# Twelve pair copies issued by SyncE in two earlier stages, and one staging tile given up for a resident pair

## The chip, the cores and the metric

The kernel runs on one core of one Trainium2 chip. The core has a matrix engine (TensorE, PE in the profile; PEld is its weight load), a vector engine (VectorE, DVE), a scalar engine (ScalarE, ACT), a general engine (GpSimd, POOL), a synchronising engine that mostly issues transfers (SyncE, SP), and 16 DMA engines that carry all transfers. The metric is the device time of one execution in microseconds (us); lower is better. It is given as the median of several runs. One more execution is taken with a profiler, and all views shown here come from such executions.

## The reference

Two independent computations are made on the same launch, and their results are put side by side. The first (A) is a state-space convolution: a four-tap shift filter along the sequence of k, times v, then a causal convolution of length 2048 per channel by way of Fourier transforms, then a product with q. The second (B) is an attention layer that carries eight memory rows from one segment of 32 rows to the next, through 64 segments.

```python
# A: S = 2048, D = 1024
for t in range(ks):
    k_shift = k_shift + k_pad[:, t:t + S, :] * shift_k[:, ks - 1 - t][None, None, :]
kv = k_shift * v
y = irfft(rfft(kv padded to 2S) * rfft(ssm_k padded to 2S))[:S] + kv * ssm_D
a = q * y
# B: 32 heads of 128, 8 memory rows, segments of 32 rows
for s in range(n_seg):
    h = jnp.concatenate([mem, xs], axis=1)
    q, k, v = h Wq, h Wk, h Wv
    p = softmax(where(mask, q k^T * scale, -1e9))
    o = (p v) Wo
    mem = o[:, :M, :]
    outs.append(o[:, M:, :])
return jnp.concatenate([a, b], axis=-1)
```

## The kernel before

All of A is computed first, and in its gaps the parts of B that do not depend on the memory rows (the projections of eight of the 32 rows of each segment, called rows in the code). Then the segment loop of B runs, one segment after the other, because each needs the memory rows of the one before.

**Weights of B.** The four weight matrices are cut into pairs of 512 KB: for Wq and Wk, the same 128 x 1024 block of both ("qk"); for Wv, two neighbouring blocks ("v"); for Wo, the rows of two heads ("o"). Not all fit into the on-chip memory (SBUF). Most pairs are resident: they are loaded once, by `res_half` (L119), two halves of 256 KB each, and stay for the whole loop. `open_res(n)` makes room for the next n of them on the left side of SBUF as the tiles of A on the right side are given back, and `load_to` (L149 for the pairs that are not resident, L119 for the resident ones) asks for the halves in the order in which the projections need them; it stops where a pair has no room yet. Two pairs are parked in PSUM. The remaining 17 pairs are streamed: they are loaded anew in every segment into a ring of five tiles, `wring` (L691). The five streamed "v" pairs are read from Wv itself. For the other 12 (seven "qk", five "o") a packed copy is first made in DRAM, `Wst`, and the ring reads that copy. The function `relay(n)` issues the copies of the next n such pairs, two transfers of 256 KB each, from DRAM to DRAM.

**Stages of A.** Times are those of the profiled execution.
1. The filter's stage, up to about 68 us. `k_iter(t)` for t = 0 to 16: the filter kernel ssm_k is transposed (PE, L450), copied to `kt`, and `stage1` of the tile before multiplies it by a table of sines and cosines (L227); ACT and DVE copy the product from PSUM into `s_sb`, and for every second t SP stores 1 MB of it into the DRAM tensor SK (L234). The tables are computed in the same time, mostly on DVE, ACT and POOL.
2. The shift products, about 68 to 165 us. A loop over t = 0, 2, ..., 16. For t below 16, DVE makes eight large operations for two rows of the sequence (L502, L506) and the product with v (L510). SP loads the k rows of a later pair (`load_k`, L251) in the middle of them and v of two rounds ahead (`load_v`, L256) after them. Then PE runs the projections of B in small portions (`rows.half`, L178 for v and L181 for q and k, with their loads on SP by `load_to`), and between them `stage1` of the products of the round before, stored into SU (L234).
3. Stage 2, about 167 to 282 us. For 17 sets, each in two halves (34 units): SP gathers the set from SK and SU (`Kg`, `Ug`, L539), PE transforms it (L567), ACT copies the filter's part (L578, L579), DVE makes the four products (L590), POOL and DVE combine them (Yre L593, Yim L594), PE transforms back (L603), ACT copies the result into a staging tile `zs` (L606), three of which take turns, and SP stores a full set into SZ (L547). Portions of `rows.half` stand between. From the unit i = 12 on, `relay(1)` is called after every second unit; its two transfers go out on POOL's queue (L128). At the end the gather tiles are given back, six more pairs are opened, and their loads follow.
4. Stage 3, about 288 to 358 us. For 16 tiles SP loads `zt` from SZ (L650) and `qt` from q (L652), PE transforms (y_ps, L668), DVE multiplies by q (L671), SP stores the result (L677). Portions of `rows.half` and their loads stand between; ACT stores the projections of a finished q and k block (QKBd, 2 MB, L189).

Then come the last projections, the parked pairs, and from about 388 us the segment loop, up to about 2060 us, and a last product with Wo.

**Order.** The program is scheduled by hand: each engine runs its instructions in the order of the program. A transfer is issued by an engine's queue in that order, too: what it has to wait for (data, a free tile, or the landing of an earlier transfer on the same one of SP's eight semaphores) holds all that stands behind it in that queue.

The lines that the change touches are the issue in `relay`, its one call in stage 2, the call `open_res(3)` ahead of stage 2 and `open_res(6)` ahead of stage 3, and the number of `zs` tiles:

```python
                zs_of[st] = wk.tile([128, 2, 1024], BF, tag="zs", name="zs", bufs=3)
            if i >= 12 and i % 2 == 0:
                relay(1)
```

Of the kernel before, what the change touches and what calls it, by code (L numbers as in the profile page):

```python
# [9 lines left out]
BF = mybir.dt.bfloat16  # L10
# [11 lines left out]
def fused_kernel(ctx: ExitStack, tc, q, k, v, shift_k, ssm_k, ssm_D, outa, x, mem0, Wq, Wk, Wv, Wo, outb, n_seg):  # L22
# [11 lines left out]
    nc = tc.nc  # L34
# [30 lines left out]
    Wst = {key: dram.tile([128, 2, 1024], BF, name=f"Wst{key[0]}{key[1]}_{key[2]}")[:] for key in relaid}  # L65
# [4 lines left out]
    def half_src(key, n):  # L70
        m, g, i = key
        if m == "qk":
            return (Wq, Wk)[n][i * 128:(i + 1) * 128, g * 1024:(g + 1) * 1024]
        if m == "v":
            return Wv[i * 128:(i + 1) * 128, (2 * g + n) * 1024:(2 * g + n + 1) * 1024]
        h = 8 * g + 2 * i + n
        return Wo[h * 128:(h + 1) * 128, :]
# [27 lines left out]
    def open_res(n):  # L105
        if n:
            pool = cw_.enter_context(tc.tile_pool(name=f"b_wres{len(to_open)}", bufs=1))
            if not wide:
                wide["t"] = pool.tile([128, 8, 2, 1024], BF, name="Wearly")
            for _ in range(n):  # L110
                res_pool[to_open.pop(0)] = pool
# [10 lines left out]
    def relay(n):  # L122

        for _ in range(n):
            if relaid:
                key = relaid.pop(0)
                for i in range(2):
                    nc.gpsimd.dma_start(Wst[key][:, i, :], half_src(key, i))  # L128


    class Rows:
# [87 lines left out]
    def stage1(u_tile, t, sbs, scratch, pool, ps_pool, by):  # L219

        if t % 2 == 0:
            sbs[0] = pool.tile([128, 2, 2, 1024], BF, tag="s1_sb", name="s1_sb")
        sb = sbs[0]
        for h in range(2):
            pt = ps_pool.tile([128, 1024], F32, tag="big", name="s1_ps")
            for hf in range(2):
                nc.tensor.matmul(pt[:, hf * 512:(hf + 1) * 512], lhsT=F1h[h][:, :],  # L227
                                 rhs=u_tile[:, hf * 512:(hf + 1) * 512], start=True, stop=True)
            if by[h] == "A":
                nc.scalar.copy(sb[:, h, t % 2, :], pt[:])  # L230
            else:
                nc.vector.tensor_copy(sb[:, h, t % 2, :], pt[:])
        if t % 2 == 1:
            nc.sync.dma_start(scratch.rearrange("m (h r) d -> m h r d", h=2)[:, :, t - 1:t + 1, :], sb[:])  # L234
# [29 lines left out]
    with ExitStack() as ck:  # L264
        ksn = ck.enter_context(tc.tile_pool(name="a_ksn", bufs=1, side="right"))
        KS = ksn.tile([128, 8, 2048], BF, name="KS_nat")
        wk = ck.enter_context(tc.tile_pool(name="a0_wk", bufs=2, side="right"))
# [178 lines left out]
        def k_iter(t):  # L446
            if t < 16:
                k_tp = ps_t.tile([128, 1024], BF, tag="tp", name="k_tp")
                for db in range(8):
                    nc.tensor.transpose(k_tp[:, db * 128:(db + 1) * 128],  # L450
                                        KS[:, db, :].rearrange("p (n r) -> p r n", r=16)[:, t, :], ident[:])
                kts[t] = wk.tile([128, 1024], BF, tag="kt", name="kt")
                if t % 2 == 0:
                    nc.scalar.copy(kts[t][:], k_tp[:])
                else:
                    nc.vector.tensor_copy(kts[t][:], k_tp[:])
                if t == 0:
                    nc.vector.tensor_tensor(out=kts[t][0:1, :], in0=kts[t][0:1, :], in1=Drow, op=ALU.add)
            if t >= 1:
                stage1(kts[t - 1], t - 1, sbs, SK1, wk, ps_big, "AD")  # L460
            if t in (8, 10, 12, 14):
                rb = t // 2 - 4
                tpx = ps_t.tile([128, 8, 128], BF, tag="tp", name="tpx")
                for kc in range(8):
                    nc.tensor.transpose(tpx[:, kc, :], XB[rb][:, kc * 128:(kc + 1) * 128], ident[:])
                nc.vector.tensor_copy(hTB[:, :, rb * 128:(rb + 1) * 128], tpx[:])
            if t >= 5:
                rows.load_to(t - 4)
# [27 lines left out]
    for t in range(0, 18, 2):  # L496
        if t < 16:
            acc = wk.tile([128, 2, 1024], BF, tag="uacc", name="uacc", bufs=1)
            pr = wk.tile([128, 2, 1024], BF, tag="prod", name="prod", bufs=1)
            for lag in (3, 2, 1, 0):  # L500
                for at, Kl in lagged(t, lag):
                    nc.vector.tensor_tensor(out=(acc if lag == 3 else pr)[:, at, :], in0=Kl,  # L502
                                            in1=SH[lag][:].unsqueeze(1).to_broadcast([128, at.stop - at.start, 1024]),
                                            op=ALU.mult)
                if lag < 3:
                    nc.vector.tensor_tensor(out=acc[:], in0=acc[:], in1=pr[:], op=ALU.add)  # L506
                else:
                    load_k(t + 4)
            u_of[t] = wk.tile([128, 2, 1024], BF, tag="u", name="u", bufs=1)
            nc.vector.tensor_tensor(out=u_of[t][:], in0=acc[:], in1=Vt[t][:], op=ALU.mult)  # L510
            load_v(t + 4)
        rows.half(2)
        for i in range(2):
            if t >= 2:
                stage1(u_of[t - 2][:, i, :], t - 2 + i, sbs, SU1, wk, ps_big, "AA" if t < 16 else "AD")
            if t < 16:
                rows.half(4 if i == 0 else 3)
            elif i == 0:
                rows.half(2)
# [5 lines left out]
    with ExitStack() as c2:  # L525
# [3 lines left out]
        ps_u = c2.enter_context(tc.tile_pool(name="a2_psu", bufs=2, space=PSUM))  # L529
        ps_k = c2.enter_context(tc.tile_pool(name="a2_psk", bufs=2, space=PSUM))  # L530

        open_res(3)

        def n_of(st):
            return 2 if st < 16 else 1
# [78 lines left out]
        zs_of = {}  # L614
        K_, U_, Y_ = {}, {}, {}
        for i in range(-1, len(hs) + 1):
            if 0 <= i < len(hs):
                st, hf = hs[i]
                if hf == 0:
                    load_set(st + 2)  # L620
                    zs_of[st] = wk.tile([128, 2, 1024], BF, tag="zs", name="zs", bufs=3)
            if i + 1 < len(hs):
                K_[i + 1] = unit_k(*hs[i + 1])
            if 0 <= i < len(hs):
                Y_[i] = unit_prod(*hs[i], K_[i], U_[i])
            rows.half(0 if i % 6 == 5 else 1)
            if i >= 1:
                unit_back(*hs[i - 1], Y_[i - 1], zs_of[hs[i - 1][0]])
            if i + 1 < len(hs):
                U_[i + 1] = unit_u(*hs[i + 1])  # L630
            if i >= 12 and i % 2 == 0:
                relay(1)
            if i + 2 == len(hs):
                cg.close()
                open_res(6)
                rows.load_to(72)
# [3 lines left out]
    with ExitStack() as c3:  # L640
        io = c3.enter_context(tc.tile_pool(name="a3_io", bufs=3, side="right"))
        wk = c3.enter_context(tc.tile_pool(name="a3_wk", bufs=2, side="right"))
        ps_big = c3.enter_context(tc.tile_pool(name="a3_ps", bufs=3, space=PSUM))
        open_res(6)
        zts = {}

        def load_z(t):
            if t < 16:
                zt = io.tile([128, 2, 1024], BF, tag="zt", name="zt")
                nc.sync.dma_start(zt[:], SZ.rearrange("m (h r) d -> r m h d", h=2)[t])  # L650
                qt = wk.tile([128, 1024], BF, tag="qt", name="qt", bufs=3)
                nc.sync.dma_start(qt[:], rows_view(q, t))  # L652
                zts[t] = zt, qt

        halves = [(key, n) for key in parked for n in range(2)]
        park_w = []
        load_z(0)
        load_z(1)
        rows.load_to(rows.at // 16 * 8 + 16)
        rows.go(4)  # L660
        for t in range(16):
            load_z(t + 2)
            rows.half(4 if t < 6 else 1)
            zt, qt = zts[t]
            pt = ps_big.tile([128, 1024], F32, tag="big", name="y_ps")
            for hf in range(2):
                for h in range(2):
                    nc.tensor.matmul(pt[:, hf * 512:(hf + 1) * 512], lhsT=G2h[h][:, :],  # L668
                                     rhs=zt[:, h, hf * 512:(hf + 1) * 512], start=(h == 0), stop=(h == 1))
            ot = wk.tile([128, 1024], BF, tag="ot", name="ot")  # L670
            nc.vector.tensor_tensor(out=ot[:], in0=pt[:], in1=qt[:], op=ALU.mult)  # L671
            if t == 14:
                rows.load_to(96)
                for key, n in halves:
                    park_w.append(pring.tile([128, 1024], BF, tag="pring", name="park_w"))
                    nc.sync.dma_start(park_w[-1][:], half_src(key, n))
            nc.sync.dma_start(rows_view(outa, t), ot[:])  # L677
# [443 lines left out]
```

## Time and profile before

| | us |
|---|---|
| median of three runs (2102.54 to 2104.24) | 2103.01 |
| profiled execution, its own time | 2093.32 |
| profiled execution, span from first to last instruction | 2091.5 |
| PE busy, share of the span | 1702.4, 81% |
| DVE busy | 1115.3, 53% |
| ACT busy | 908.7, 43% |
| POOL busy | 413.1, 20% |
| DMA, share of the 16 engines' time in the three large queues | 88.8%, 3.3%, 2.1% |
| granted TensorE clock, mean | 0.984 |

The page divides the span into 40 equal slices of about 52 us; a digit is the busy share in tenths:

```profile
PE   5888987888788888888887878888888878888879
DVE  6986833355555555555555555555555555555541
POOL 2004730121111111111111111111212121111110
DMA  6899989999999999999999999999999999999980
```

The first seven slices are A with the projections of B between its steps; the 32 after the eighth are the segment loop, in which the DMA engines are in use nine tenths of the time or more. A group of instructions on the page reads: line, engine, operation, what it writes and reads, shapes and count, then its busy time, the mean ns of one, and the idle time of the engine just before them with what ended most of it. "SPq" is SP's queue of transfers; such a row tells when a transfer was issued, not when it was done. The copies of the streamed pairs have these rows among the transfers (out<-in, issuer, count, size, median us from issue to landing):

```profile
Wsto<-in_B_Wo_dram POOLq DMA_DIRECT2D x10, 256.0 KB, 3.8
...
Wstqk<-in_B_Wq_dram POOLq DMA_DIRECT2D x7, 256.0 KB, 5.5
Wstqk<-in_B_Wk_dram POOLq DMA_DIRECT2D x7, 256.0 KB, 6.2
```

### The profile page before, as it was taken

How to read it: one execution, taken by the hardware profiler on the slowest of the kernel's cores; microseconds unless marked ns; L12 is line 12 of the kernel's file. 1: busy time of each engine (PE TensorE's matmuls, PEld its weight loads, DVE VectorE, ACT ScalarE, POOL GpSimd, SP SyncE). 2: the span in 40 equal slices, each digit the busy share in tenths (PEclk: the TensorE clock that was granted, in tenths of full speed). 3: DMA queues.
4: the chain of work that ended last, by engine and by line, in shares of the span. 5: the costliest groups of instructions: out<-in, count | busy, mean ns of one | idle time of the engine just before them, and what ended most of it. 6: DMA issues, size and time to landing. Idle time of an engine off the chain costs nothing. (4 is left out here: it accounts for less than half of the span.)

```text
span 2091.5 us, 73911 instructions
## 1 busy us (share of the span) xinstructions
PE 1702.4 (81%) x30484; PEld 894.2 (43%) x30514; DVE 1115.3 (53%) x3313; ACT 908.7 (43%) x2276; POOL 413.1 (20%) x1018
## 2 busy tenths in 40 slices
PE   5888987888788888888887878888888878888879
PEld 2433233444444444444444444444444444444449
DVE  6986833355555555555555555555555555555541
ACT  5556731244444444444444444444444444444430
POOL 2004730121111111111111111111212121111110
PEclk9999999999999999999999999999999999999999
DMA  6899989999999999999999999999999999999980
GB/s 236 282 346 362 343 287 381 352 377 372 356 375 368 365 360 370 372 366 375 358 368 353 367 358 372 359 377 358 371 358 378 363 352 351 374 370 379 368 337 23
DMA packets 266384, 728.64 MB, mean 348 GB/s; under 512 B 65007, under 2 KB 77183, under 8 KB 265277
## 3 DMA queue, kind: packets, MB, share of 16 engines
q1 hardware_dynamic: 239486, 686.65, 88.8%
q0 software_dynamic: 15520, 22.06, 3.3%
q10 hardware_dynamic: 11040, 15.21, 2.1%
q8 instruction: 239, 3.92, 0.7%
q14 instruction: 99, 0.81, 0.1%
HBM read 673.52 MB, written 56.56 MB: 349 GB/s over the span
## 5 line engine op out<-in xcount | busy, mean ns | idle before, releaser
L795 PE MATMUL qkacc<-Wqk,hT 128*32 128x512 bf16 x4096 | 338.5, 383 | 0.0
L795 PEld LDWEIGHTS <-hT 128*32 128x32 bf16 x8192 | 184.9, 96 | 236.3 <-issue 84.2
L916 PEld LDWEIGHTS <-OT 128*32 128x32 bf16 x8192 | 210.1, 96 | 109.5 <-issue 59.2
L795 PE MATMUL qkacc<-wring,hT 128*32 128x512 bf16 x2048 | 204.9, 389 | 31.3 <-DMA wring<-Wstqk 25.5
L763 DVE COPY wring<-park 128x1024 bf16<-128x1024 bf16 x128 | 88.6, 692 | 239.4 <-PE vacc L809 124.8
L875 ACT ACTIVATE P<-S 128x128 bf16<-128x128 f32 x256 | 71.1, 278 | 330.4 <-DVE S L867 244.3
L809 PE MATMUL vacc<-Wv,hT 128*32 128x512 bf16 x2560 | 209.8, 382 | 0.0
L809 PE MATMUL vacc<-wring,hT 128*32 128x512 bf16 x1536 | 154.7, 387 | 65.5 <-DMA wring<-in_B_Wv_dram 63.6
L809 PEld LDWEIGHTS <-hT 128*32 128x32 bf16 x4096 | 113.0, 95 | 184.4 <-issue 108.3
L762 ACT COPY wring<-park 128x1024 bf16<-128x1024 bf16 x128 | 130.7, 1021 | 138.9 <-PE qkacc L795 112.8
L894 DVE COPY PB<-P 32x160 bf16<-32x160 bf16 x896 | 172.9, 193 | 10.6
L879 DVE TENSOR_REDUCE sm<-P 128x4 f32<-128x256 bf16 x256 | 107.5, 420 | 128.6 <-ACT P L876 128.6
L831 ACT COPY QK<-tp 128x256 bf16<-128x256 bf16 x256 | 95.4, 373 | 185.7 <-PE tp L822 184.5
L795 PE MATMUL qkacc<-Wearly,hT 128*32 128x512 bf16 x2048 | 161.0, 391 | 18.4 <-DVE hT L936 17.9
L830 POOL COPY QK<-qkb 128x64 bf16<-128x64 bf16 x256 | 61.3, 239 | 564.5 <-PE tp L822 404.8
L916 PE MATMUL yacc<-wring,OT 128*32 128x256 bf16 x2520 | 126.7, 274 | 37.4 <-DMA wring<-Wsto 35.2
L905 ACT CAST OT<-otacc 128x256 bf16<-128x256 f32 x256 | 98.7, 386 | 130.4 <-PE otacc L901 130.4
L801 ACT CAST qks<-qkacc 128x512 bf16<-128x512 f32 x256 | 151.1, 590 | 4.2 <-PE qkacc L795 3.5
L1030 POOL DMA_DIRECT2D out_dram<-Y_sb x256 | 129.1, 511 | 84.8 <-ACT Y_sb L1026 82.8
L822 PE MATMUL tp<-ident,qks 128*128 128x128 bf16 x1024 | 102.4, 223 | 52.6 <-ACT qks L801 50.3
L866 DVE TENSOR_REDUCE mx<-S 128x4 f32<-128x160 f32 x256 | 83.2, 325 | 85.2 <-PE S L863 79.5
L901 PE MATMUL otacc<-PB,vsb 128*128 128x160 bf16 x512 | 97.6, 238 | 35.3 <-ACT vsb L816 35.3
(212 smaller groups left out, 2957.1 us busy)
## 6 DMA issues: line engine op xcount, KB each, us to landing
wring<-Wstqk SPq DMA_DIRECT2D x448, 512.0 KB, 6.2
wring<-in_B_Wv_dram SPq DMA_DIRECT2D x320, 512.0 KB, 6.7
wring<-Wsto SPq DMA_DIRECT2D x315, 512.0 KB, 6.3
SK<-s_sb SPq DMA_DIRECT2D x8, 1024.0 KB, 5.5
SU<-s_sb SPq DMA_DIRECT2D x8, 1024.0 KB, 8.9
QKBd<-stq ACTq DMA_DIRECT2D x4, 2048.0 KB, 9.5
Kg<-SK SPq DMA_DIRECT2D x16, 512.0 KB, 7.0
Ug<-SU SPq DMA_DIRECT2D x16, 512.0 KB, 8.3
```

The lines of the kernel that those rows point to most:

```text
L762: nc.scalar.copy(t[:, 0, :], park[key][0][:])
L795: nc.tensor.matmul(u.qk[p0:p0 + 32, :], lhsT=hT[:, kc, :], rhs=w[:, t, c2 * 512:(c2 + 1) * 512], start=(kc == 0), stop=(kc == 7), tile_pos ...
L801: nc.scalar.copy(u.qks[:], u.qk[:])
L809: nc.tensor.matmul(vacc[0][32 * c:32 * c + 32, :].rearrange("p (n x) -> p n x", n=2), lhsT=hT[:, kc, :], rhs=w[:, :, c * 256:(c + 1) * 256 ...
L822: nc.tensor.transpose(tp[:, j * 128:(j + 1) * 128], src[:, j * 128:(j + 1) * 128], ident[:])
L831: nc.scalar.copy(u.QT.rearrange("e (c j) r -> e c j r", c=2), tv[:, 0])
L879: nc.vector.tensor_reduce(out=sm[:], in_=Pv.rearrange("p b x k -> p x b k"), op=ALU.add, axis=AX.XY)
L894: (nc.vector if by[c] == "D" else nc.gpsimd).tensor_copy(to, src)
L901: nc.tensor.matmul(o, lhsT=w[:, i * 128:(i + 1) * 128], rhs=PB[:, 2 * kb + i].rearrange("p c q -> p (c q)"), start=(kb == 0), stop=(kb == 1))
L905: nc.scalar.copy(u.OT[:].rearrange("e (c i) q -> e i c q", i=2), ov[:, :, :, 0:32])
L916: nc.tensor.matmul(Y[32 * dq:32 * dq + 32, 0:256], lhsT=u.OT[:, hh, 0:32], rhs=w[:, hh % 2, dq * 256:(dq + 1) * 256], start=(u.g == 0 and ...
L1030: nc.gpsimd.dma_start(outb[32 * s:32 * s + 24, dq * 256:(dq + 1) * 256], Y_sb[32 * dq + 8:32 * dq + 32, :])
```

## The change

The copies are issued by SP. The call in stage 2 goes. In the filter's stage `relay(2)` is called at t = 1, 2, 3 and 4 (eight pairs, 16 transfers: the seven "qk" pairs and one "o" pair); in the shift products `relay(1)` is called at t = 2, 4, 6 and 8, after the first two portions of projections and ahead of `stage1` (four "o" pairs, eight transfers). Stage 2 has two `zs` tiles instead of three, which leaves 4 KB per partition; one more pair is opened ahead of stage 2, and one less ahead of stage 3. The loads of the pair that is opened earlier move with it: one half of a resident "v" pair and one block for `pring`, which stood behind it in `load_to`'s order, are now asked in the middle of stage 2.

```diff
@@ relay
                 for i in range(2):
-                    nc.gpsimd.dma_start(Wst[key][:, i, :], half_src(key, i))
+                    nc.sync.dma_start(Wst[key][:, i, :], half_src(key, i))
@@ k_iter (the filter's stage)
             if t >= 1:
                 stage1(kts[t - 1], t - 1, sbs, SK1, wk, ps_big, "AD")
+            if 1 <= t <= 4:
+                relay(2)
@@ shift products
         rows.half(2)
+        if 2 <= t <= 8:
+            relay(1)
         for i in range(2):
@@ stage 2
-        open_res(3)
+        open_res(4)
...
-                    zs_of[st] = wk.tile([128, 2, 1024], BF, tag="zs", name="zs", bufs=3)
+                    zs_of[st] = wk.tile([128, 2, 1024], BF, tag="zs", name="zs", bufs=2)
...
-            if i >= 12 and i % 2 == 0:
-                relay(1)
@@ stage 3
-        open_res(6)
+        open_res(5)
```

## The prediction

> **What bounds the kernel now.** I read the page's slices and groups first, then busy time by stage, then the waits and the order of events in the first 390 us, where the change lies. The last part of the kernel, the segment loop, takes 388 to 2060:
>
> ```profile
> span 2091.5 us, 73911 instructions
> L795 PE MATMUL qkacc<-wring,hT 128*32 128x512 bf16 x2048 | 204.9, 389 | 31.3 <-DMA wring<-Wstqk 25.5
> L809 PE MATMUL vacc<-wring,hT 128*32 128x512 bf16 x1536 | 154.7, 387 | 65.5 <-DMA wring<-in_B_Wv_dram 63.6
> ```
>
> The streamed pairs (wring) are what the TensorE waits for in the loop: it is paced by transfers. The change leaves the loop's transfers as they are, so whatever is won or lost before it moves its start and is neither mended nor multiplied there. Next, busy time by stage (columns: stretch and its us; busy us of PE, PE weight load, DVE, ACT, POOL with instructions; granted PE clock; share of the DMA engines in use; GB/s).
>
> ```profile
> 30.00:45.00 15.00, 7.52 (x45) 4.62 (x44) 12.20 (x26) 7.37 (x10) 10.02 (x16) 0.76 0.39 151
> 75.00:89.00 14.00, 11.78 (x54) 5.15 (x54) 13.60 (x13) 6.68 (x10) 0.00 (x0) 1.00 0.49 163
> 89.00:104.00 15.00, 14.61 (x67) 6.59 (x68) 14.60 (x13) 9.90 (x14) 0.00 (x0) 1.00 0.92 300
> 104.00:129.00 25.00, 18.20 (x79) 7.52 (x77) 22.80 (x21) 11.53 (x16) 3.23 (x4) 0.95 1.03 409
> 214.00:262.00 48.00, 43.95 (x244) 13.75 (x248) 42.78 (x73) 38.27 (x71) 36.05 (x42) 1.00 1.01 349
> 278.00:290.00 12.00, 10.94 (x48) 4.46 (x49) 1.63 (x3) 4.10 (x7) 3.28 (x4) 1.00 0.94 312
> 324.00:356.00 32.00, 18.13 (x77) 6.91 (x79) 11.98 (x10) 2.93 (x5) 0.00 (x0) 1.00 1.03 378
> ```
>
> The filter's stage (to 68 us) has free DMA time at 30 to 45. The shift products (68 to 165) have it only until their own loads start at 89; from then to 129 the transfers are saturated. Stage 2 (167 to 282) moves as much, but see its waits below. Stage 3 is saturated again while the PE is half idle: 324 to 356 is bound by bytes. Now what the PE waits for at the end of the saturated stretch, from the waits of 75 to 170 us, and the timelines of PE and SP there:
>
> ```profile
> PE ps_q L181 <- DMA pring<-in_B_Wq_dram: 4.2, 1, 4.2
> PE ps_q L181 <- DMA Wqk<-in_B_Wq_dram: 1.4, 2, 1.0
> ```
> ```profile
> 124.03 0.39 PE L181 MATMUL ps_q<-hTB,Wqk 128*128 128x512 bf16 x1 [0.40 <-DMA Wqk<-in_B_Wq_dram]
> 128.58 0.61 PE L181 MATMUL ps_q<-hTB,pring 128*128 128x512 bf16 x1 [4.16 <-DMA pring<-in_B_Wq_dram]
> 129.21 0.61 PE L181 MATMUL ps_q<-hTB,Wqk 128*128 128x512 bf16 x1
> ```
> ```profile
> 119.15 1.03 SPq L149 DMA_DIRECT2D pring<-in_B_Wq_dram  x1
> 120.23 0.50 SPq L119 DMA_DIRECT2D Wqk<-in_B_Wq_dram  x1
> ```
>
> The pring request of 119.15 lands after 9.4 us (128.5), the Wqk request behind it after 8.9 (129.1): both sat in a full queue, and the PE stood still for them. From 129.2 to 170 the PE is busy without a gap (30.89 of 31 us in 134 to 165), so a later restart is later stage 2 and 3.
>
> **The change, part by part.** 24 copies of 256 KB (12 pairs, two halves) leave POOL and go to SP: 16 into the filter's stage, 8 into the shift products.
>
> *Price of one copy.* The rows nearest are POOL's own copies when little else moves: asked 0.52 us apart at 265.8 and 266.3, they land after 2.9 and 3.0 us, so 0.6 apart; at 270.1 and 270.6 after 3.0 and 3.4, 0.9 apart. At 409 GB/s (row above) 256 KB of plain load take 0.64. A copy asked by SP is in no row; bounds 0.6 and 0.95, and I take the middle of the two pairs, 0.75. The pair at 276.6, beside other loads, gives 2.9 and 4.1: 1.7 apart, kept as the far bound.
>
> *16 copies in the filter's stage: 0.* Four follow SP's last input load (19.25) and finish before the SK store of 29.58. Eight follow that store, which lands at 34.4; with 8 × 0.75 = 6.0 the queue is clear at 40.4, and the next store (38.90, held by DVE s_sb) would start to move about 2 us after its issue. Four follow it: 40.9 + 2.9 for the 1 MB + 3.0 = 46.8, and Wearly's 0.64 makes 47.4, while the store of 45.96 moves from about 48. Cover: the idle DMA of 30 to 45. Without it: at 0.95 the eight end at 42.0, the store at 44.9, the four at 48.7, Wearly at 49.3, 1.3 late; from there s_sb waits for SK landings (three times, 5.7 us in all), so it would be paid in full. Bounds 0 and +1.3; a gain is excluded, nothing there waits for POOL's copies.
>
> *8 copies among the shift products: +6.0.* Two each at t = 2, 4, 6, 8: behind the pring requests of 89.06 and 99.01, the Wearly request of 109.03 and the pring request of 119.15. Behind them on SP stand the weights, the SU stores, and the k and v loads. SP's own time for the issues (0.33 to 0.5 us each) lies in its waits for DVE u before v loads, 35.0 us in all; it also waits for earlier landings before it asks again, which moves its requests but not the order of a full queue. DVE takes 10.0 us per pair of products and asks k and v a round ahead, so those keep slack. The weights do not: all eight copies stand ahead of the Wqk of 120.23, in a queue with share 0.92 to 1.03. 8 × 0.75 = 6.0 later restart. Bounds: 8 × 0.61 = 4.9, less 15 × 0.08 = 1.2 if the gaps of 89 to 104 take some: 3.7; and 8 × 0.95 = 7.6. After the standstill the PE's clock is low (matmul 0.61 for 0.38 us) until 133.4. After the wait of 4.33 us that ended at 301.9 it was low for 5.5 us, so I add nothing for a longer wait.
>
> *Copies out of stage 2: 0.* POOL loses 24 × 0.53 = 12.7 us of issue. Its cover: POOL waits for DVE pb before Yre (22.7 us in 187 to 262), and the pace of 6.07 us per two units is the same before 214, when no copy is issued. No wait there names a transfer. Only at 265.75 does POOL run without a gap, after its memsets; the PE's wait for Yre (1.82, ended 265.86) comes ahead of it. Bounds 0 and −1.0.
>
> *Two staging tiles: 0.* A zs tile is rewritten 7.75 us or more after its store is asked (215.20, 223.31; 221.34, 229.09); stores of 214 to 262 land in 6.0 to 6.7 us. If that 1.0 us were gone, ACT would wait before zs, and PE's z_ps slots behind it.
>
> *Lighter 278 to 290: −1.7.* Four of POOL's copies and two loads (one Wv and one pring, now asked in the middle of stage 2 thanks to the pair opened there) leave this stretch: 6 × 0.66 = 4.0 us of DMA time. But stage 3's first zt request waits for the last SZ store, asked by ACT at 282.02 when its unit is done; it lands 6.2 us later, in the full queue. Six loads still stand before it; the 64 KB H loads in the loop, at share 0.98, land in 4.9, ol's 32 KB in 2.5 when idle. I take 4.5: zt 1.7 sooner, and the rest of the 4.0 is idle DMA. Bounds 0 and −4.0.
>
> Sum: 0 + 6.0 + 0 + 0 − 1.7 = **+4.3 us**. It is made in the profiled execution (span 2091.5, device time 2093.32); the runs' median is 2103.01, 9.7 higher for the same program, and I add the difference to it: 2107.3.
>
> **Rivals.** *It cancels (2104.0).* Copies at 0.61, 1.2 us of them in the gaps of 89 to 104, and 2.7 of the 4.0 kept at stage 3: 4.9 − 1.2 − 2.7 = +1.0. For it: share 0.92 there. Against: SP holds several requests in flight, so these gaps need not be an empty queue.
>
> *Stage 3 opens in time (2098.5, faster).* At 289.03 ACT asks a 2 MB store (QKBd). The zt of 289.51 behind it lands after 12.4 us, the PE waits 1.03 and 4.33, and its clock is low for about 13 matmuls at 0.43 instead of 0.216 a piece: 2.8 more, 8.2 in all. If the last SZ store lands before 286.5, the first two zt and qt (1.5 MB, 4 us) are ahead of that store. With 3.7 lost earlier: −4.5. Against: 324 to 356 runs at share 1.03, so a PE that is ahead waits there.
>
> *Copies cost double (2116.7).* A copy reads and writes the chip's memory; two shares of 0.64 are 1.28. Then the filter's eight end at 34.4 + 10.2 = 44.6, the store at 47.5, the four at 52.6, Wearly at 53.2: 5.2 late; 10.2 in the shift products; −1.7: +13.7. Against: 0.6 and 0.9 between landings. The Trainium skill (DMA: Bandwidth & Descriptors, Specifications) limits a core to about 358 GB/s of this memory. By that limit a copy of 256 KB read and 256 KB written is an estimated 1.46 us, and the sum an estimated 8 × 1.46 − 1.7 = +10.0 before the filter's stage; the 409 GB/s of the row and the landings 0.6 apart do not bear it out, hence the small chance.
>
> **How the numbers follow.** Forecast 0.57 (own range 2103.5 to 2111), cancels 0.20, faster 0.15, double 0.08. About 0.2% (4.2 us) is what a measurement of this kernel can tell from no change. Slower by more: 0.42 of the forecast's 0.57, whose bounds reach further up than down, and 0.08: 0.50. Within: 0.15 + 0.20 = 0.35. Faster: 0.15. The likeliest time is 2107.3; the range 2099 to 2114 takes in both bounds of a copy and reaches to the faster rival.
>
> **What would show it.** In the changed profile the PE's wait in front of ps_q near 122 to 135 is about 10 to 12 us instead of 5.6, stage 2's first gather asked near 173 instead of 167.2, its pace still 6.07 per two units, and the first zt asked near 292.5 instead of 288.25. SK stores of 45.96 to 68.70 stay put; if they slip, the copies are dearer. If ps_q restarts before 132, the queue had room and I am wrong there; if y_ps does not wait for the second zt and stage 3's end (y_ps at 354.76) comes under 355, the faster rival holds. An ACT wait before zs on an SZ landing would refute the staging term.

## The result, and the profile after

The changed kernel takes 2111.25 us (median of 13 runs), the kernel before 2102.54 in the same comparison (13 runs): ratio 1.0052, 95% interval 1.0028 to 1.0076, so 6 to 16 us slower. The profiled execution of the changed kernel took 2104.6 us of device time. These lines of its page answer to the three shown first of the kernel before (span, and the two groups of matmuls that wait for streamed pairs):

```profile
span 2102.8 us, 73935 instructions
L797 PE MATMUL qkacc<-wring,hT 128*32 128x512 bf16 x2048 | 208.1, 395 | 25.5 <-DMA wring<-Wstqk 20.1
L811 PE MATMUL vacc<-wring,hT 128*32 128x512 bf16 x1536 | 154.2, 390 | 68.2 <-DMA wring<-in_B_Wv_dram 67.0
```

The loop waits as before: 93.7 us in these two groups, 96.8 before. The span is 11.3 longer, and 9.1 of that is there when the loop starts. The table follows the delay from its beginning, by the start of one instruction at each place. The last column is the kernel before, unchanged, profiled once more (an experiment below); it tells how far such places wander by themselves. The second k block is taken by its first matmul.

| start of | before, us | after, us | difference | unchanged kernel again |
|---|---|---|---|---|
| first shift product (DVE uacc) | 68.55 | 73.64 | +5.09 | +0.35 |
| second k block (PE ps_k) | 146.14 | 156.22 | +10.08 | -0.36 |
| first product of stage 2 (DVE pa) | 175.81 | 186.81 | +11.00 | +0.14 |
| its 21st product | 235.68 | 247.04 | +11.36 | -0.16 |
| its last product | 277.15 | 287.43 | +10.28 | -0.22 |
| first zt load of stage 3 | 288.25 | 296.76 | +8.52 | -0.33 |
| last y_ps product | 355.42 | 364.52 | +9.11 | 0.00 |
| segment loop | 388.47 | 397.58 | +9.11 | +0.01 |

Two places make it: the filter's stage (+5.1) and the shift products (+5.0). Stage 2 adds 1.3 up to its 21st product and gives 1.1 back at its end, stage 3's opening gives back 1.8, and 0.6 of that is lost again by the last y_ps.

Busy time by stage, first of the kernel before for one stretch not shown yet, then of the changed kernel (columns as in the prediction):

```profile
45.00:75.00 30.00, 25.08 (x170) 14.27 (x173) 25.37 (x42) 16.77 (x20) 0.00 (x0) 0.95 0.94 322
```
```profile
30.00:45.00 15.00, 7.54 (x46) 4.66 (x45) 12.24 (x26) 7.53 (x10) 9.99 (x16) 0.75 0.90 270
45.00:75.00 30.00, 21.98 (x149) 12.86 (x149) 20.54 (x37) 14.87 (x16) 0.00 (x0) 0.84 0.88 303
104.00:129.00 25.00, 21.04 (x95) 9.13 (x94) 24.30 (x23) 12.40 (x17) 2.47 (x3) 1.00 1.02 398
```

At 30 to 45 the engines do what they did before (DVE 12.2, ACT 7.5), so nothing is late yet; the DMA share has gone from 0.39 to 0.90, but at 270 GB/s, where a share of 1.02 moves 398 in the third row. The transfers are in use and slow. At 45 to 75 DVE does 20.5 us of work for 25.4: here the time is lost. The waits of 20 to 110 us tell for what, first before, then after (us in total, times, longest):

```profile
ACT s_sb L230 <- DMA SK<-s_sb: 5.7, 3, 2.0
...
DVE s_sb L232 <- DMA SK<-s_sb: 0.2, 1, 0.2
```
```profile
ACT s_sb L230 <- DMA SK<-s_sb: 10.6, 4, 6.1
...
DVE s_sb L232 <- DMA SK<-s_sb: 6.4, 2, 4.4
```

The largest wait stands in ACT's timeline of the changed kernel:

```profile
49.08 1.03 ACT L230 CAST s_sb<-s_ps 128x1024 bf16<-128x1024 f32 x1
56.17 1.01 ACT L230 CAST s_sb<-s_ps 128x1024 bf16<-128x1024 f32 x1 [6.05 <-DMA SK<-s_sb]
```

s_sb has two tiles. The tile needed at 50.1 is free when the third SK store has landed. These are that store's request and the time to its landing, first before, then after:

```profile
45.96 0.52 SPq L234 DMA_DIRECT2D SK<-s_sb  x1
...
DMA to landing us min/median/max: 5.0/5.0/5.0
```
```profile
45.79 0.57 SPq L234 DMA_DIRECT2D SK<-s_sb  x1
...
DMA to landing us min/median/max: 10.3/10.3/10.3
```

It lands at 56.07 instead of 50.96, 5.1 us later, as much as the first shift product is late. It is not asked later; it waits in SP's queue behind the copies. By the landings of the single transfers, the first four copies follow the last input load (25.81) and end at 28.45, 0.66 each. The eight behind the first SK store take 34.99 to 43.96, 1.12 each. The four behind the second store (two "qk", two "o") take 47.17 to about 53.0, 1.46 each; the last one's landing is not in the trace, the load behind it lands at 53.60.

Among the shift products the PE waits for weights in front of ps_q, as predicted (timeline of the changed kernel; before it was 1.03, 0.40 and 4.16 between 123 and 128.6):

```profile
133.07 1.28 PE L181 MATMUL ps_q<-hTB,Wqk 128*128 128x512 bf16 x2 [2.80 <-DMA Wqk<-in_B_Wq_dram]
136.97 0.61 PE L181 MATMUL ps_q<-hTB,pring 128*128 128x512 bf16 x1 [2.62 <-DMA pring<-in_B_Wq_dram]
139.47 0.61 PE L181 MATMUL ps_q<-hTB,Wqk 128*128 128x512 bf16 x1 [1.89 <-DMA Wqk<-in_B_Wq_dram]
```

But these waits are 7.3 us instead of 5.6, only 1.7 of the 5.0. A further 2.2 are lost earlier, in front of ps_v, where waits for transfers come to 3.1 us instead of 0.9:

```profile
108.65 0.38 PE L178 MATMUL ps_v<-pring,hTB 128*128 128x512 bf16 x1 [1.28 <-DMA KR<-in_A_k_dram]
112.53 0.38 PE L178 MATMUL ps_v<-Wv,hTB 128*128 128x512 bf16 x1 [1.55 <-DMA Wv<-in_B_Wv_dram]
```

The remaining 1.1 is in no wait for a transfer. The granted clock between the two places is 0.94 instead of 0.96, so slower matmuls are likely, but this was not isolated.

And the opening of stage 3, SP's requests and the PE's wait:

```profile
296.76 0.59 SPq L652 DMA_DIRECT2D zt<-SZ  x1
297.46 0.53 SPq L654 DMA_DIRECT2D qt<-in_A_q_dram  x1
298.05 0.56 SPq L652 DMA_DIRECT2D zt<-SZ  x1
```
```profile
310.36 1.76 PE L670 MATMUL y_ps<-zt,G2h 128*128 128x512 bf16 x4 [3.93 <-DMA zt<-SZ]
```

The first zt is asked 9.3 us after the last product of stage 2 (before 11.1). The second is asked at 298.05, this time 1.3 ahead of ACT's 2 MB store (QKBd, 299.31), and still lands only after 12.3 us: the PE waits 3.9 us for it, before 4.3.

### The profile page after: what moved, and what is told of

Same layout as the page of the kernel before. It is cut to its first block, busy times and chain, and to the rows that moved or that the text cites. A ratio compares the mean times of both kernels' runs of the same rounds, so it can differ in the third digit from the quotient of the medians.

```text
span 2102.8 us, 73935 instructions
## 1 busy us (share of the span) xinstructions
PE 1712.4 (81%) x30514; PEld 895.5 (43%) x30514; DVE 1114.5 (53%) x3313; ACT 909.8 (43%) x2276; POOL 399.4 (19%) x994
## 5 line engine op out<-in xcount | busy, mean ns | idle before, releaser
L797 PE MATMUL qkacc<-Wearly,hT 128*32 128x512 bf16 x2048 | 169.3, 409 | 18.4 <-DVE hT L938 17.9
L1032 POOL DMA_DIRECT2D out_dram<-Y_sb x256 | 128.6, 509 | 90.8 <-ACT Y_sb L1028 86.6
```

The lines of the kernel that those rows point to most:

```text
L797: nc.tensor.matmul(u.qk[p0:p0 + 32, :], lhsT=hT[:, kc, :], rhs=w[:, t, c2 * 512:(c2 + 1) * 512], start=(kc == 0), stop=(kc == 7), tile_pos ...
L1032: nc.gpsimd.dma_start(outb[32 * s:32 * s + 24, dq * 256:(dq + 1) * 256], Y_sb[32 * dq + 8:32 * dq + 32, :])
```

## Experiments

In these edits `relay` has been given the queue to use; the rooms of the change (two zs tiles, `open_res(4)`, `open_res(5)`) are in all kernels but the unchanged one. Places are in us, differences to 68.55, 146.14 and 355.42 of the kernel before. Some of the expectations take 146.6 for the second k block of the kernel before, which is its third matmul and not its first; where they say that the shift products lost 4.6 us, it is 5.0. The comparisons of one set share the runs of the kernel before: 2094.84 (25 runs) for the first four, 2095.16 (29 runs) for the last three with a ratio.

**The parts alone.** First the filter's stage alone; the pairs not copied there are issued by POOL at the end of stage 2:

```diff
-        if 2 <= t <= 8:
-            relay(1)
...
+            if i >= 28 and i % 2 == 0:
+                relay(1, nc.gpsimd)
```

> The 16 copies of the filter's stage stay on SP; the eight of the shift products go back to POOL in stage 2 (units 28 to 34). The changed kernel lost 5.1 us before the first shift product (68.5 to 73.6) and a further 4.6 by the second k block (146.6 to 156.2). Theory A (the copies of the filter's stage hold up the SK stores): the first shift product again starts near 73.6, and nothing more is lost after it, so the second k block starts near 151.7 and the last y_ps near 359 (before: 355.4; changed: 364.5). Theory B (the filter's stage was late for another reason, the copies only stand there): first shift product near 68.5.

Ratio 1.0084 [1.0053, 1.0115] (4 runs); first shift product 74.89 (+6.3), second k block +5.9, last y_ps 361.28 (+5.9). The filter's copies alone make a delay that stays.

Then the shift products alone, with the four last pairs ("o", as in the changed kernel):

```diff
-            if 1 <= t <= 4:
-                relay(2)
...
-            relay(1)
+            relay(1, nc.sync, -1)
...
+            if i >= 12 and i % 2 == 0:
+                relay(1, nc.gpsimd)
```

> The eight copies among the shift products stay on SP; the other eight pairs are copied by POOL in stage 2 as before the change. Theory A: first shift product at 68.5, second k block 4.6 to 5.5 us late (151 to 152), since eight copies at about 0.65 us stand ahead of the Wqk load that the PE waits for; the last y_ps near 359. Theory B: the shift products are late only because the filter's stage left a full queue behind, and the second k block starts within 1.5 us of 146.6.

Ratio 1.0037 [1.0015, 1.0060] (10 runs); first shift product 68.54, second k block 152.00 (+5.9), last y_ps 360.04 (+4.6). At the last y_ps the two parts come near to the whole: 5.9 + 4.6 = 10.5, with 9.1 in the changed kernel.

Then the rooms alone, all copies where they were:

```diff
-                    nc.sync.dma_start(Wst[key][:, i, :], half_src(key, i))
+                    nc.gpsimd.dma_start(Wst[key][:, i, :], half_src(key, i))
...
+            if i >= 12 and i % 2 == 0:
+                relay(1)
```

> All copies as before the change; only the two staging tiles and the pair opened earlier. Theory A: no ACT wait before zs on a store, the milestones up to the last unit of stage 2 within 0.3 us of before, the first zt request 0 to 0.7 us earlier (two loads fewer ahead of the last SZ store). Rival: the third staging tile was needed, stage 2's pace of 6.07 us per two units gets longer, and the last unit (277.2 before) is 1 us or more late.

Ratio 1.0017 [0.9995, 1.0039] (10 runs); last y_ps 353.75 (-1.7), and no ACT wait in front of zs that names a transfer. The staging tile was free to give up. The places ahead were expected within 0.3 and were not: first shift product 69.21 (+0.7), second k block 145.25 (-0.9), last product of stage 2 276.14 (-1.0). Up to stage 2 this program is the one before, so a single profile wanders by up to about 1 us at such places, more than the unchanged kernel's second profile shows.

The way from the last product of stage 2 to the first zt tells what the copies at the end of stage 2 cost. It takes 11.1 us in the kernel before and 12.0 here. In the four kernels without copies there (the changed one, the shift products alone, the three early pairs below, and the changed one with three tiles below) it takes 9.3 to 9.7, in all ten others 10.4 to 12.0. So the gain there is from the copies, not from the loads that the extra pair moved. That it reaches the end is not shown: from the last product to the last y_ps the four take 77.0 to 78.7, the ten 77.0 to 78.9.

Only three pairs early, ahead of the first SK store:

```diff
-            if 1 <= t <= 4:
-                relay(2)
+            if t == 1:
+                relay(3)
...
-        if 2 <= t <= 8:
-            relay(1)
...
+            if i >= 12 and i % 2 == 0:
+                relay(1, nc.gpsimd)
```

> Three pairs are copied by SP at t = 1 of the filter's stage, in the gap before the first SK store (six copies, 25.8 to about 29.7 us at 0.65); the other nine by POOL in stage 2 from unit 12 on, so the last three pairs' copies (265 to 281) are gone from its end. If a copy in an empty queue costs 0.65 and only copies behind a store cost more: first shift product within 0.3 us of 68.5, second k block within 0.3 of 146.6, last unit of stage 2 0 to 1 us earlier than 277.2, first zt request 1 to 3 us earlier than 288.25, last y_ps 1 to 3 us earlier than 355.4. If copies delay the filter's stage wherever they stand: first shift product 1 to 2 us late.

First shift product 68.65, first zt 285.37 (-2.9) and last y_ps 353.78 (-1.6) are as expected; the second k block (144.99) and the last product of stage 2 (275.87) are 1.2 and 1.3 early, not within 0.3 and 1, much as with the rooms alone. The loop starts at 388.48 (before 388.47). But the ratio is 1.0055 [1.0027, 1.0083] (10 runs). Nothing ahead of the loop accounts for that; the next run asks what such a ratio is worth.

**The unchanged kernel, measured as a variant.**

> The kernel before, unchanged, measured as the variants are. Theory A (single executions of the segment loop wander by several us, and that is all that the variants show beyond their shift of the loop's start): ratio 1.000 within its interval, first shift product, second k block and last y_ps within 0.5 of 68.55, 146.57 and 355.42, while the loop's length may differ from 1641 by up to 10. Theory B (a kernel that is not the reference of the comparison comes out slower by place or order): ratio above 1.002.

Ratio 1.0020 [1.0003, 1.0038] (12 runs), at the edge of theory B: an unchanged kernel came out 0.2% slower, and 1.000 lies just outside the interval. The places of the table above repeat within 0.4 us, as theory A has it; the span does not, and by more than the 10 us that it allowed. Lines of its page:

```profile
span 2114.3 us, 73941 instructions
L795 PE MATMUL qkacc<-wring,hT 128*32 128x512 bf16 x2048 | 209.0, 397 | 27.0 <-DMA wring<-Wstqk 22.3
L809 PE MATMUL vacc<-wring,hT 128*32 128x512 bf16 x1536 | 154.8, 390 | 72.5 <-DMA wring<-in_B_Wv_dram 71.1
```

and the loop by itself, first the first profile, then this one:

```profile
388.00:2029.00 1641.00, 1332.64 (x27900) 709.09 (x27900) 858.03 (x2944) 720.92 (x1985) 313.64 (x896) 0.99 0.99 367
```
```profile
388.00:2029.00 1641.00, 1327.07 (x27516) 703.01 (x27516) 846.47 (x2901) 711.98 (x1956) 308.42 (x884) 0.98 0.98 361
```

In the same 1641 us the same program moved 361 GB/s instead of 367 and got less far: its loop is 22.4 us longer (from 388.5 to 2051.9 instead of 2029.6). The loop's length wanders from one execution to the next by more than all that is studied here. The granted clock is lower as well (0.984 over the first profile's span, 0.975 over this one's); which follows from which is not shown. So a difference of a few us is to be read from the places ahead of the loop, and a ratio of 1.002 is not told from no change by itself. Against the unchanged kernel's ratio, taken in another set, the change's 1.0052 is 0.0032 more, 6.7 us (plus or minus 6, from the two intervals); the 9.1 at the loop's start are 0.0043. The two agree, but the ratios of the variants do not follow the loop's start closely (three early pairs: 1.0055 at +0.0; the filter's copies alone: 1.0084 at +5.9). What is shown is the delay at the loop's start; that it is all of the measured slowing is not.

**What is dear about the filter's copies.** These kernels have no copies among the shift products. All 16 ahead of the first SK store, the last four pairs by POOL late in stage 2:

```diff
-            if 1 <= t <= 4:
-                relay(2)
+            if t == 1:
+                relay(8)
```

> All 16 copies of the filter's stage are asked in one go at t = 1, ahead of the first SK store; none stands behind a store. The other eight (four o pairs) are issued by POOL late in stage 2. Theory A (a copy costs 0.63 us in a queue that holds nothing else, and 1.1 and more only between SK stores): the 16 land between about 25.8 and 36, the first SK store near 39, the third lands by 52, the first shift product starts at 68.5 to 69.5 (before 68.55, all 16 spread over t = 1 to 4: 74.9). Theory B (a copy costs 1.1 to 1.4 wherever it stands, as reading and writing share the memory): the 16 land by 42 to 45, the first SK store near 47, and the first shift product starts at 73 or later.

2116.04 us (one run). First shift product 73.43 (+4.9); the copies land from 26.96 to 43.63 with no store between them, and the first SK store is asked only at 36.59, since SP asks for copies until 34.93. Theory A falls: it is not the stores that make the copies dear. The 14 "qk" halves take 26.96 to 42.34, 13 steps of 1.18; the two "o" halves at the end follow 0.64 apart.

Plain stores, then plain loads of the same size in the copies' places (here and in the run after them the twelve pairs are copied by POOL in stage 2, as in the kernel before):

```diff
-                relay(2)
+                for n in range(4):
+                    nc.sync.dma_start(Wdup[t - 1, n], KR[:, 2 * (n % 2), :])
```

> In the filter's stage SP asks 16 plain stores of 256 KB (on-chip tile to DRAM, result unused) in the places of the 16 copies; all copies are issued by POOL in stage 2. If the write side is what makes copies dear between SK stores: they land 1.1 us and more apart behind the first SK store and the first shift product starts near 74, as with copies (74.9). If read and write together are what is dear: 0.65 apart, first shift product within 1.0 of 68.55.

```diff
-                relay(2)
+                for n in range(4):
+                    nc.sync.dma_start(dup[:, n, :], half_src(("qk", t - 1, n), n % 2))
```

> In the filter's stage SP asks 16 plain loads of 256 KB (the same rows of Wq and Wk into an on-chip tile, result unused) in the places of the 16 copies; all copies are issued by POOL in stage 2. If the read side were what makes copies dear: near 74. If the writes, or both together, are: loads land 0.64 apart and the first shift product starts within 1.0 of 68.55.

Stores: first shift product 68.49, nothing lost, landings mostly 0.6 apart. Loads: 70.61 (+2.1, between the two outcomes that were expected), the third SK store landing at 53.38. So the write side alone is free and the read side alone costs a third of the 6.3. (The loads' four tiles made SP ask for the later ones only when earlier ones had landed, so their spacing is not a clean price.)

Copies again, but from a contiguous source: rows of Wo as in an "o" pair, where a "qk" half takes 2 KB out of each 8 KB row:

```diff
-                relay(2)
+                for n in range(4):
+                    nc.sync.dma_start(Wdup[t - 1, n // 2][:, n % 2, :], half_src(("o", t - 1, n // 2), n % 2))
```

> In the places of the 16 copies of the filter's stage, 16 copies of 256 KB whose source is contiguous (Wo rows, as an o pair's) into packed scratch tiles of the same form; the real copies by POOL in stage 2. If the source's stride makes copies dear (the seven qk pairs read 2 KB pieces 8 KB apart): they land 0.64 apart and the first shift product starts at 68.5 to 69.5. If a copy as such is dear once more than a few stand in the queue: about 1.1 apart on average, first shift product at 73 or later.

First shift product 68.90 (+0.3, as much as the unchanged kernel's own second profile). The eight behind the first SK store land from 35.85 to 41.59: 0.72 each instead of 1.12. At 30 to 45, the kernel with the filter's copies alone first, then this one:

```profile
30.00:45.00 15.00, 7.25 (x46) 4.33 (x45) 12.53 (x29) 7.00 (x9) 10.00 (x16) 0.89 0.84 240
```
```profile
30.00:45.00 15.00, 7.81 (x46) 4.64 (x44) 12.14 (x27) 7.18 (x9) 10.03 (x16) 0.77 0.96 312
```

240 against 312 GB/s: what is copied, from where to where, sets the price. The contiguous copies read and write other tensors too, so the source's form is the likely part, not an isolated one. (Further on this kernel falls behind again, last y_ps 357.15, +1.7; that was not pursued.)

**What turns a late store into lost time.** The kernel with the filter's copies alone, but with three s_sb tiles in the filter's stage:

```diff
-            sbs[0] = pool.tile([128, 2, 2, 1024], BF, tag="s1_sb", name="s1_sb")
+            sbs[0] = pool.tile([128, 2, 2, 1024], BF, tag="s1_sb", name="s1_sb", bufs=bufs)
...
-                stage1(kts[t - 1], t - 1, sbs, SK1, wk, ps_big, "AD")
+                stage1(kts[t - 1], t - 1, sbs, SK1, wk, ps_big, "AD", 3)
```

> The 16 copies stay at t = 1 to 4 in the filter's stage, but s_sb has three tiles instead of two there, so that ACT and DVE need not wait for the landing of the store before the last; the other eight copies by POOL late in stage 2. Theory A (what is lost is the wait for an s_sb tile; the queue catches up by 60 us): most of the 6.3 us goes, first shift product at 69 to 71. Theory B (the transfers themselves are behind until 68 us): it stays at 73 or later, with the wait moved to a later s_sb tile.

First shift product 67.53, where 69 to 71 was expected: not only the 6.3 are gone, it is 1.0 ahead of the kernel before; last y_ps 353.89 (-1.5). No wait for an SK landing is left, though the third store still lands late (54.83). The stretch that lost time:

```profile
45.00:75.00 30.00, 25.96 (x173) 14.18 (x175) 25.95 (x42) 16.73 (x19) 0.00 (x0) 0.96 1.01 371
```

DVE is back at 25.95 us of work and the transfers run at 371 GB/s: once nobody waits for it the queue catches up (the eighth SK store lands at 74.92, before at 74.35). (Its one time, 2116.64, has a loop of 1665.7 us, 24.6 longer than the first profile's, as the unchanged kernel's second one was.)

The changed kernel with three tiles, and the rooms alone with three tiles:

> The changed kernel with three s_sb tiles in the filter's stage instead of two. If the stage's loss is only the wait for an s_sb tile: first shift product at 67 to 68 (changed kernel 73.64), what is left is the loss among the shift products, second k block near 151.5, last y_ps at 358 to 360.5 (changed kernel 364.52), ratio to the kernel before 1.001 to 1.003. If the two losses share one cause in the queue, the shift products lose more than the 4.6 and last y_ps stays above 362.

> Copies as in the kernel before (POOL, stage 2), the change's rooms (two zs tiles, the pair opened earlier), and three s_sb tiles in the filter's stage. If the kernel before, too, loses in the waits for an s_sb tile (5.7 us of ACT): first shift product at 64 to 67, last y_ps at 350 to 353, ratio 0.997 to 0.999. If DVE is the next bound right behind: first shift product at 67.5, as with the copies and three tiles, last y_ps near 353, ratio 0.999 to 1.001.

The changed kernel with three tiles: first shift product 68.35, second k block 151.25 (+5.1), last y_ps 361.10 (+5.7; 358 to 360.5 was expected), ratio 1.0022 [1.0003, 1.0042] (12 runs), which cannot be told from the unchanged kernel's 1.0020. The filter's loss is gone, the shift products' stays. The rooms with three tiles: first shift product 67.60, as expected if DVE is the next bound, so the wait for s_sb of the kernel before was worth about 1.0, as much as such places wander; last y_ps 355.28 (near 353 was expected), ratio 1.0015 [0.9993, 1.0037]. No variant was measured faster than the kernel before.

## Why the prediction came out as it did

The direction and the second of the two places were right, and 2111.25 is inside the range of 2099 to 2114, above the 2107.3 that was named. The sum of the steps, +4.3, was half of what came (+9.1 at the loop's start). One step was outside its bounds, and the time is in the range because the range was wide, not because the sum was right.

- **16 copies in the filter's stage: 0, bounds 0 and +1.3. Measured +5.1. This is the step that failed.** The cover was named rightly (idle DMA at 30 to 45), but the price of a copy, 0.6 to 0.95, was read from POOL's copies at 265 to 270, which are all "o" halves, and 14 of these 16 are "qk" halves. At 1.12 for the eight and 1.46 for the four behind them, the third SK store lands 5.1 late; and as the prediction said for that case, a late store is paid in full, because s_sb waits for landings (a third tile takes the loss away). The trace had rows for "qk" copies: in stage 2 of the kernel before, the two halves of the seven "qk" pairs land 1.78, 1.66, 1.42, 0.93, 0.82, 1.74 and 1.46 us apart, and the listing of transfers gave medians of 5.5 and 6.2 us beside 3.8. These rows were a warning and no proof, for they stand in a busier place: the one "o" pair in the same stretch lands 0.99 apart, two later ones 1.77 and 1.84.
- **8 copies among the shift products: +6.0, bounds 3.7 and 7.6. Measured +5.0** (second k block against first shift product; 5.3 with three tiles, 5.9 alone). The size held. These are "o" halves, and so did their price: the six that stand in a full queue take 0.62 to 1.17 and together 4.45 us, 0.74 each. The first two (landing at 100.89 and 101.87) stood in the gaps of 89 to 104, and little is left for them. The place was only partly right: the sum has all of it in front of ps_q and adds nothing for the clock, but only 1.7 of the 5.0 are there; 2.2 are in front of ps_v, and 1.1 in no wait for a transfer, at a lower granted clock.
- **Copies out of stage 2: 0, bounds 0 and -1.0.** Between its 21st and its last product the changed kernel gains 1.1, but the copies are not the reason: with three tiles and no copies in stage 2 either, these products take 41.4 us as in the kernel before (41.5), and two kernels with copies there, the 16 ahead and the plain loads, take 40.4 as the changed one does. The pace is the same: ten units take 29.99 us, before 29.98. What makes the 1.1 stayed open.
- **Two staging tiles: 0.** Right; ACT's waits in front of zs name no transfer.
- **Lighter 278 to 290: -1.7. Measured -1.8** from the last product to the first zt, and by the way it was predicted: the last SZ store lands after 4.4 us (4.5 was taken, 6.2 before). By the parts alone it comes from the copies and not from the two loads. In the changed kernel 1.2 of it is left at the last y_ps; over all kernels no such gain is seen there.
- Not in the sum: +1.3 from the second k block to the 21st product of stage 2. The unchanged kernel has 0.2 there. The PE's waits for the gathers at the opening are 5.1 us instead of 3.9, but kernels with shorter waits show such a loss too; it was not pursued.

Of the rivals, "copies cost double" had the filter's stage to 0.1 us (5.2), by 1.28 a copy, and missed the shift products (10.2 for 5.0): neither price was the price of all copies, so the hit is in part luck. It rested beside a limit that the Trainium skill gives (DMA: Bandwidth & Descriptors, Specifications: about 358 GB/s of this memory for a core, by which a copy was an estimated 1.46). The traces bear this limit out for neither kind as a rule: "o" copies at 0.72 read and write 728 GB/s together, "qk" copies at 1.12 read and write 468. The Trainium skill says on the same page, in its section Bandwidth, that this limit is the share when both cores of a pair stream, and gives more than it for one core alone; the 398 GB/s of 104 to 129 agree. "Stage 3 opens in time" expected that a zt asked ahead of the 2 MB store would land in time; the second zt was asked 1.3 us ahead of it and was as late as before.

Of the signs named in advance, "SK stores of 45.96 to 68.70 stay put; if they slip, the copies are dearer" failed and pointed at the reason: from the fifth on they are asked 5 to 6 us late (the eighth at 73.78). The 10 to 12 us of waiting in front of ps_q did not come either (7.3). Stage 2's first gather (176.93 for 173) and the first zt (296.76 for 292.5) are 3.9 and 4.3 later than forecast, since the filter's 5.1 were not in it.

## What to carry to other kernels

Look for the price of a transfer in rows of the same transfer (same source, same form) as well, even if they lie in a busier place: the quietest row may be of another kind, and where the two differ, the bounds must take in both. Idle transfer time covers work only if what is queued behind may come late; count the tiles that wait for a landing, since in the filter's stage one more tile was worth all that the copies cost. And measure the unchanged kernel as a variant before a difference of a few tenths of a per cent is explained.

## What was not expected of the hardware

- Copies from one place of the chip's memory to another cost 0.72 us per 256 KB from a contiguous source and 1.12 from 2 KB pieces of 8 KB rows, eight of each in the same stretch and queue; yet the first four of either kind, behind the input loads, land 0.6 to 0.7 apart in these two kernels. Why the strided ones slow down only later stayed open. Single packets go with it: from 35 to 44 us of the changed kernel 59 of 867 packets of 2 KB take 300 to 960 ns, where most take 84; while the eight contiguous copies land it is 7 of 782.
- The loop of one and the same program took 1641.1 and 1663.4 us in two profiled executions, at 367 and 361 GB/s. What sets this is not shown here; nor is why three early pairs gave 1.0055 with a loop that starts on time.
